# Fused attention and max-of-two projection on one core: a new order for the first part of the work, w2's first part loaded second and transposed ahead of the first pair's last scores

## The chip, the cores and the metric

One core of one Trainium2 chip. The metric is device time in microseconds of one execution; the median of three runs before the change is 329.46 us (329.17 to 329.52).

## The reference

```python
batch, n_heads, seq, head_dim = (8, 12, 448, 64)
scores = scale * np.matmul(q, k.transpose(0, 1, 3, 2))
scores = cap * np.tanh(scores / cap)
scores = scores - np.max(scores, axis=-1, keepdims=True)
attn = np.exp(scores)
attn = attn / (np.sum(attn, axis=-1, keepdims=True) + 1e-09)
attn_out = np.matmul(attn, v)
x = attn_out.transpose(0, 2, 1, 3).reshape(B * S, H * D)
h1 = x @ w1
h2 = x @ w2
g = np.maximum(h1, h2)
return g @ w_out
```

x is 3584 x 768, w1 and w2 are 768 x 1024, w_out is 1024 x 768, all given as float32. The cap is 30, so the exponentials stay small enough to be taken without the maximum, and the kernel leaves that subtraction out.

## The kernel before

The kernel computes in bfloat16 with sums in float32. It uses max(h1, h2) = relu(h1 - h2) + h2: with wd = w1 - w2 (`wd_sb`) and wm = w2 @ w_out (`wm_sb`), the result is relu(x @ wd) @ w_out + x @ wm. The product wm is made in the kernel, out of transposed pieces of w2.

The whole program is one list of steps, `ORDER` (lines 9 to 203), read by the loop at line 742. Each engine gets its instructions in the order in which they stand there and works them off in that order; a step that waits holds all later steps of its own engine. Nothing reorders them. GpSimd's queue (POOL) issues nearly all loads, converting to bfloat16; SyncE (SP) and ScalarE (ACT) issue the four plain loads of the first two pairs; SyncE also issues the transposing DMAs and the stores. A load from GpSimd also waits for the landing of the load eight places ahead of it.

Heads are worked in pairs (48 of them, pair i) and quads (t, pairs 2t and 2t + 1). One step is a name and its numbers:

- `ld0`, `cd`: plain loads of k and q of pairs 0 and 1, and their casts. `lk i`, `lq i`, `lv t`: loads of k, q and v from GpSimd (lines 317 and 336). `lw2 c`, `lw1 c`, `lwo`: parts of w2, w1, w_out (lines 364, 389, 357).
- `dm`, `ms0`, `ms`, `id`: VectorE (DVE) memsets of `warm`, of `ident`, of `ones` and its kin; `id` is GpSimd's affine select that makes `ident` the identity.
- `D bank n`: filler matmuls on `warm` (`keep_warm`, line 465), n units of 128 columns in instructions of up to 512.
- `X i bank` and `Xh`: TensorE transposes of k and q of pair i (L458), moved to SBUF by VectorE with `XC`, `XCh` (L463). `W c bank`: transposes of w2's part c (L416), moved with `WC` (L420).
- `S i j`: scores of pair i, keys 128 j to 128 j + 127 (L514); `L t`: the 64 keys left over, for the quad (L528). `T`, `TL`: tanh of these on ScalarE (L519, L532). `E i j0 j1`, `EL`: the exponentials (L536, L539).
- `OP c half bank`, `P c half n`: n matmuls of the premultiplication wm (L431); `PC`: its result to SBUF (L437). `sub c e`: wd = w1 - w2 (L402).
- `Y t bank`: sums of the exponentials (L566, L570, from quad 3 on L573, after the adds `A`, `B` on VectorE); `Y1`, `Y2`, `Y3`: their inverse. `VL t`, `V t u j0 j1`: the values (L600, L606); `N t u`: normalised into `xT` (L618, L621).
- `O g bank`, `M a b n`: open a group of the projection in a bank, and n steps of group a on the upper and b on the lower half of the rows of the array (L645; -1 is no group). `ev`, `eva`: the group's result to SBUF (L666, L702). `H`, `Hs`: a bank changes hands between the halves. `st`: store. `cr t`: DMA transpose of k and q from quad 5 on (L475).

Scores go to two PSUM tiles in turn, `s0` and `s1`, which `VL` and `V` share; the order of turns is line 503. A score step therefore waits for the tanh that empties its tile. The other four banks, mm0 to mm3, are named in the steps. For quad 0 the tiles are, in the order of the list: S 0 1 in s1, S 0 0 and S 0 2 in s0, L 0 and S 1 0 in s1, S 1 2 in s0, S 1 1 in s1. k and q of two quads (`kqs`) and v of two (`vp`) are held at a time, so a load waits until the quad two before has been used.

Before the change TensorE has, up to the first P: X 0, X 1, S 0 1, S 0 0, L 0, S 0 2, W 2, S 1 0, X 3, X 2, S 1 2, S 1 1, W 3, W 1, S 2 1, S 2 0, with D between. GpSimd's first loads are lk 3, lk 2, lq 3, lq 2, lw2 2, lw2 3, lw2 1, two of lwo, lv 0 1, lw2 0, lv 0 0.

Of the kernel before, what the change touches and what calls it, by code (L numbers as in the profile page):

```python
# [39 lines left out]
A 5 0 1; A 5 0 2; ev 8; ev 9; M 11 10 7; S 12 1; lk 17 1; M 11 10 4; T 12 0; lq 17 0; O 12 2; M 12 10 1; A 5 1 1;  # L40
M 12 10 1; Hs 11; cr 7; M 12 10 1; M 12 11 1; B 5 0; M 12 11 1; T 12 1; M 12 11 1; S 12 2; H 10 2; B 5 1;
M 10 11 1; T 12 2; M 10 11 5; E 11 2 3; st 0 0; M 10 11 2; O 13 0; M 13 11 1; ev 10; L 6; VL 5; A 5 1 2; TL 6;
V 5 0 0 2; V 5 1 0 2; Y 5 3; E 12 0 3; V 5 0 2 3; V 5 1 2 3; Y1 5; S 13 0; M 13 11 1; lv 7 0; M 13 11 1; Y2 5;
M 13 12 2; Y3 5; M 13 12 1; lv 7 1; M 13 12 3; N 5 0; M 13 12 1; lv 7 2; M 13 12 1; T 13 0; M 13 12 1; N 5 1;
M 13 12 1; lv 7 3; M 13 12 1; O 14 3; M 14 12 2; EL 6; Hs 13; S 13 1; lk 18 0; M 14 12 1; M 14 13 1; ev 11;
M 14 13 1; Hs 12 2; T 13 1; S 13 2; lk 18 1; M 14 13 1; A 6 0 1; M 12 13 2; T 13 2; Hs 14; M 12 13 1; lq 18 0;
A 6 0 2; S 14 0; M 12 13 3; E 13 0 2; M 12 13 1; S 14 1; lk 19 0; M 12 13 1; O 15 1; M 15 13 2; ev 12; M 15 13 1;
lk 19 1; M 15 14 2; ev 13; M 15 14 1; T 14 0; O 16 2; M 16 14 1; lq 19 0; A 6 1 1; M 16 14 1; st 0 1; M 16 14 1;
Hs 15; T 14 1; cr 8; B 6 0; M 16 15 1; S 14 2; M 16 15 1; ev 14; M 16 15 1; T 14 2; O 17 0; M 17 15 2; H 16;
M 17 15 1; B 6 1; M 17 16 2; E 13 2 3; M 17 16 1; ev 15; O 18 3; M 18 16 1; L 7; VL 6; A 6 1 2; st 0 2; TL 7;  # L50
V 6 0 0 2; V 6 1 0 2; Y 6 1; E 14 0 3; V 6 0 2 3; V 6 1 2 3; Y1 6; S 15 0; M 18 16 1; lv 8 0; M 18 16 1; Y2 6;
M 18 17 1; Y3 6; M 18 17 1; lv 8 1; M 18 17 1; O 19 1; M 19 17 2; ev 16; Hs 18; lv 8 2; M 19 17 1; M 19 18 1;
T 15 0; N 6 0; M 19 18 2; lv 8 3; O 20 2; M 20 18 2; EL 7; Hs 19; ev 17; M 20 18 1; lk 20 0; S 15 1; M 20 19 1;
N 6 1; M 20 19 1; T 15 1; M 20 19 1; lk 20 1; O 21 0; M 21 19 3; Hs 20; M 21 20 1; lq 20 0; ev 18; M 21 20 1;
S 15 2; S 16 0; ev 19; M 21 20 1; T 15 2; O 22 3; M 22 20 1; lk 21 0; M 22 20 1; A 7 0 1; Hs 21; M 22 20 1;
M 22 21 1; E 15 0 2; M 22 21 1; lk 21 1; ev 20; S 16 1; M 22 21 1; O 23 1; M 23 21 1; A 7 0 2; M 23 21 1; Hs 22;
lq 21 0; M 23 21 1; M 23 22 2; ev 21; M 23 22 1; T 16 0; M 23 22 2; A 7 1 1; M 23 22 2; cr 9; M 23 22 1; T 16 1;
M 23 22 1; B 7 0; S 16 2; M 23 22 2; B 7 1; O 24 2; M 24 22 1; T 16 2; M 24 22 2; H 23; M 24 23 1; H 22 2;
E 15 2 3; M 24 23 2; M 22 23 1; L 8; VL 7; A 7 1 2; TL 8; V 7 0 0 2; V 7 1 0 2; Y 7 0; E 16 0 3; V 7 0 2 3;
# [719 lines left out]
```

## Time and profile before

| | us |
|---|---|
| median of 3 runs | 329.46 |
| lowest, highest | 329.17, 329.52 |
| the profiled execution | 329.59 |
| its span in the trace | 327.8 |

The profile is of one execution. PE is TensorE's matmul, PEld its weight loads, DVE VectorE, ACT ScalarE, POOL GpSimd, SP SyncE. A timeline row is start, length, engine, line, operation, output and input, count, and in brackets the idle time before it with what ended it. L numbers are lines of this kernel. Times within the span start at its begin; the difference between the profiled execution's time and its span lies outside of the trace. Ends of matmuls are modelled, and a row with a length of several instructions runs from the first's start to the last's end.

### The profile page before, as it was taken

What the parts mean: (1) busy time and instruction counts of PE and PEld (TensorE: products, weight loads), DVE (VectorE), ACT (ScalarE), POOL (GpSimd) and SP (SyncE); (2) the same over time, 40 slices, a digit from 0 to 9 for tenths busy, and PEclk for the clock granted to TensorE, in tenths of its full rate; (3) what the DMA queues carried; (4) which work ended last, traced back from release to release, by engine and by line L of the source; (5) the groups of instructions that cost most, each with busy time, mean ns of one, the idle gap of its engine ahead of it and who ended that gap; (6) DMA issues with size and microseconds to landing.
All of it is one profiled execution on the core that took longest, in us unless ns stands there. A gap on an engine that the chain in (4) does not pass through costs nothing.

```text
span 327.8 us, 9768 instructions
## 1 busy us (share of the span) xinstructions
PE 320.3 (98%) x4137; PEld 184.6 (56%) x4140; DVE 240.2 (73%) x422; ACT 281.2 (86%) x278; POOL 161.7 (49%) x237
## 2 busy tenths in 40 slices
PE   8899999999999999999999999999999999999994
...
ACT  5899999999999999999999999999999999921120
...
GB/s 186 193 201 134 289 185 168 115 127 137 202 187 102 118 193 194 123 79 170 165 184 90 212 138 184 109 177 142 188 114 90 211 154 46 2 50 98 0 98 96
DMA packets 134507, 46.28 MB, mean 141 GB/s; under 512 B 112320, under 2 KB 129472, under 8 KB 134464
## 3 DMA queue, kind: packets, MB, share of 16 engines
...
q8 instruction: 32, 0.52, 0.7%
q10 hardware_dynamic: 448, 0.66, 0.5%
...
## 4 chain that ended last, share of the span: by engine, by line
PE 86%; DVE 6%; DMA 6%; POOL 1%; issue 1%; POOLq 0%; DVEq 0%
PE mm L645 58%; PE s L514 8%; PE s L606 8%; DMA w2b<-in_moe_w_dram 3%; PE mm L431 3%; DMA osb<-in_moe_w_dram 2%; PE s L528 2%; PE mm L573 1%; PE mm L640 1%; PE s L600 1%; DVE wd_sb L402 1%; PE mm L416 1%; DVE gT L666 1%; DVE xT L621 1%; POOL kqs L321 1%; PE mm L458 1%
## 5 line engine op out<-in xcount | busy, mean ns | idle before, releaser
L519 ACT ACTIVATE e<-s 128x896 bf16<-128x896 f32 x144 | 125.8, 928 | 6.3 <-PE s L514 6.0
L536 ACT ACTIVATE e<-e 128x1792 bf16<-128x1792 bf16 (+2 forms) x72 | 123.2, 1712 | 0.0
L645 PE MATMUL mm<-wo_sb,gT 64*128 64x384 bf16 x864 | 115.5, 323 | 0.0
L645 PE MATMUL mm<-wm_sb,xT 64*128 64x384 bf16 x648 | 101.9, 323 | 0.1
L645 PE MATMUL mm<-xT,wd_sb 64*128 64x448 bf16 x768 | 97.2, 350 | 0.0
L328 POOL DMA_DIRECT2D kqs<-in_k_dram x76 | 54.7, 721 | 54.0 <-DMA qkT<-kqs 49.9
L645 PEld LDWEIGHTS <-gT 64*128 64x128 bf16 x864 | 58.7, 94 | 25.4 <-issue 1.1
L645 PEld LDWEIGHTS <-wd_sb 64*128 64x128 bf16 x768 | 48.9, 94 | 27.2 <-issue 2.4
L645 PEld LDWEIGHTS <-xT 64*128 64x128 bf16 x648 | 50.5, 94 | 18.3 <-issue 0.2
L514 PE MATMUL s<-qkT 64*128 64x448 bf16 x288 | 51.8, 352 | 0.0
L352 POOL DMA_DIRECT2D vp<-in_v_dram x48 | 30.6, 642 | 34.3 <-PE s L514 26.4
L666 DVE TENSOR_SCALAR gT<-mm 128x448 bf16<-128x448 f32 x64 | 38.9, 617 | 8.6 <-PE mm L645 7.6
L328 POOL DMA_DIRECT2D kqs<-in_q_dram x38 | 35.1, 925 | 5.9 <-PE mm L458 5.0
L606 PE MATMUL s<-e,vp 128*32 128x448 bf16 x576 | 36.0, 354 | 0.0
L548 DVE TENSOR_TENSOR esum<-e 128x896 bf16<-128x896 bf16 x42 | 26.0, 618 | 9.9 <-ACT e L536 9.9
L621 DVE TENSOR_TENSOR xT<-s,inv 64x448 bf16<-64x448 f32 x48 | 29.9, 622 | 0.9
L548 DVE TENSOR_TENSOR esum<-esum,e 128x896 bf16<-128x896 bf16 x42 | 26.2, 623 | 5.8 <-ACT e L536 4.8
L514 PEld LDWEIGHTS <-qkT 64*128 64x128 bf16 x288 | 18.4, 94 | 19.2 <-issue 11.0
L700 ACT COPY osb<-mm 128x384 f32<-128x384 f32 x10 | 4.8, 478 | 26.9 <-PE mm L645 26.7
L702 DVE COPY osb<-mm 128x384 f32<-128x384 f32 x44 | 23.3, 554 | 5.0 <-PE mm L645 4.5
L553 DVE TENSOR_TENSOR esum<-esum,el 64x896 bf16<-64x896 bf16 x42 | 26.0, 619 | 1.2
L578 DVE STREAM_TRANSPOSE st<-mm 128x448 f32<-128x448 f32 x24 | 15.6, 649 | 13.2 <-PE mm L573 11.6
...
## 6 DMA issues: line engine op xcount, KB each, us to landing
...
kqs<-in_q_dram POOLq DMA_DIRECT2D x46, 112.0 KB, 5.6
...
w2b<-in_moe_w_dram POOLq DMA_DIRECT2D x6, 256.0 KB, 6.8
...
vp<-in_v_dram POOLq DMA_DIRECT2D x10, 128.0 KB, 6.8
```

What stands on the lines that cost most here:

```text
L328: nc.gpsimd.dma_start(out=to, in_=x)
L352: nc.gpsimd.dma_start(out=to, in_=x)
L514: scored[i, j] = nc.tensor.matmul(s[:, h, :S], k_of(t, o, h, j), q_of(t, o, h)).ins
L519: nc.scalar.activation(expo[i][:, 2 * j : 2 * j + 2, :], slots[i, j][:, :, :S], AF.Tanh, scale=scale / cap)
L536: nc.scalar.activation(e, e, AF.Exp, scale=float(cap))
L548: nc.vector.tensor_add(d, e[:, 0:2, :] if j == 1 else d, e[:, 2 * j : 2 * j + 2, :])
L553: nc.vector.tensor_add(d, d, left_e[t][r, :, :])
L606: nc.tensor.matmul(vals[t][place(m, u), u, :S], w[:, m, :], expo[2 * t + o][:, 2 * j + h, :], start=False, stop=(j == NJ - 1))
L621: nc.vector.tensor_mul(x[64 - r : 128 - r], vals[t][r : r + 64, u, :S], sums[t, 3][64 - r : 128 - r])
L645: ins = nc.tensor.matmul(self.ps, w[r], x[r], start=first, stop=self.at == [self.n, self.n]).ins
L666: nc.vector.tensor_relu(gT[b // 2][:, f, cs], ps)
L702: nc.vector.tensor_copy(o[:, hs], ps)
```

## The change

Only `ORDER` changes. Up to the opening of the projection's twelfth group the steps stand in another order; no step of the computation is added or taken away there. The filler goes from 104 units (28 instructions) to 96 (26). `lw2 3` is GpSimd's second transfer, and `W 3` stands ahead of `S 0 2`; `ms` stands ahead of `dm` and `ms0`, and `id` ahead of GpSimd's first load. Some steps get another bank. After that point banks 0 and 2 are exchanged in many of the `O` and `Y` steps, and nothing else differs. The new list has one line more, so that line numbers behind it grow by one.

```diff
-ld0 k; ld0 k 1; ld0 q; ld0 q 1; dm; ms0; lk 3 0; lk 2 0; lq 3 0; id; D 3 8; ms; cd q; cd k; lq 2 0; lw2 2; lw2 3;
-lw2 1; D 3 24; Xh 0 0 0; Xh 0 1; cd k 1 1; cd q 1 1; XCh 0 1; XCh 0 0; D 3 5; X 1 1; S 0 1; S 0 0; XC 1; T 0 1;
-T 0 0; D 0 5; D 1 12; L 0; D 1 8; S 0 2; W 2 0; TL 0; T 0 2; S 1 0; X 3 2; D 1 26; X 2 1; S 1 2; T 1 0; E 0 0 3;
-T 1 2; lwo 0 0; lwo 0 1; lv 0 1; lw2 0; lv 0 0; lk 5 0; lq 5 0; lq 4 0; lk 4 0; lwo 1 0; lv 1 1; lwo 1 1; WC 2;
-XC 3; XC 2; S 1 1; W 3 3; W 1 2; D 0 16; S 2 1; WC 1; WC 3; T 1 1; E 1 2 3; T 2 1; S 2 0; OP 1 0 1; P 1 0 1;
-OP 3 0 3; P 3 0 3; OP 2 0 0; P 2 0 3; P 1 0 1; P 2 0 1; P 1 0 2; L 1; P 3 0 1; P 1 0 2; P 3 0 1; P 2 0 1; P 1 0 1;
-P 3 0 1; P 2 0 3; P 3 0 2; PC 3 0; PC 2 0; T 2 0; E 1 0 2; TL 1; EL 0; S 2 2; S 3 0; Y 0 2; P 1 0 1; W 0 0; T 2 2;
-T 3 0; VL 0; V 0 0 0 3; V 0 1 0 3; S 3 1; X 4 3; lv 1 0; lk 8 0; lw2 5; lq 6 0; lk 7 0; lk 6 0; lw2 4; lq 8 0;
-lw1 4; lq 7 0; lw1 2; lw1 0; lv 2 1; lv 2 0; WC 0; Y1 0; Y2 0; PC 1 0; Y3 0; XC 4; N 0 0; N 0 1; E 2 0 3; T 3 1;
-EL 1; E 3 0 2; X 5 0; OP 0 0 2; P 0 0 5; OP 1 1 3; P 1 1 4; P 0 0 1; OP 2 1 1; P 2 1 3; S 4 0; S 3 2; P 0 0 1;
-P 2 1 2; P 0 0 1; P 1 1 3; P 2 1 3; P 1 1 1; XC 5; PC 0 0; PC 2 1; PC 1 1; T 3 2; T 4 0; E 3 2 3; OP 3 1 2;
-P 3 1 2; S 4 1; S 4 2; Y 1 1; T 4 1; T 4 2; L 2; P 3 1 4; VL 1; V 1 0 0 3; V 1 1 0 3; TL 2; E 4 0 3; S 5 0;
-P 3 1 2; W 4 3; T 5 0; EL 2; Y1 1; Y2 1; Y3 1; N 1 0; N 1 1; WC 4; PC 3 1; X 6 1; X 8 0; S 5 1; S 5 2; W 5 2;
-XC 8; XC 6; sub 4 0; WC 5; T 5 1; T 5 2; OP 4 0 0; P 4 0 8; S 6 0; X 7 1; OP 0 1 3; P 0 1 8; S 6 1; E 5 0 2;
-T 6 0; E 5 2 3; T 6 1; PC 4 0; XC 7; sub 2 0; PC 0 1; S 6 2; OP 5 1 1; P 5 1 7; L 3; T 6 2; TL 3; E 6 0 3; Y 2 3;
-VL 2; V 2 0 0 3; V 2 1 0 3; S 7 0; OP 5 0 2; P 5 0 1; P 5 1 1; P 5 0 7; sub 0 0; Y1 2; Y2 2; Y3 2; N 2 0; N 2 1;
-PC 5 1; A 3 0 1; PC 5 0; T 7 0; EL 3; lw1 1; lk 9 0; lq 10 0; lk 11 0; lw1 3; lq 9 0; lk 11 1; lv 3 1; lq 11 0;
-lv 4 0; lv 3 0; lk 10 0; lw1 5; lk 10 1; O 0 0; M 0 -1 1; S 7 2; S 7 1; O 1 3; M 1 -1 1; M 0 -1 3; M 1 -1 1;
-M 0 -1 2; T 7 1; T 7 2; Hs 0; S 8 0; M 1 -1 1; M 1 0 3; S 8 1; X 9 2; OP 4 1 1; P 4 1 4; sub 1 0; sub 3 0; XC 9;
-E 7 0 2; T 8 1; T 8 0; P 4 1 4; L 4; O 2 2; M 2 0 2; S 8 2; M 2 0 1; M 2 1 3; A 3 0 2; A 3 1 1; B 3 1; PC 4 1;
-ev 0; B 3 0; Hs 2; TL 4; E 7 2 3; T 8 2; S 9 0; O 3 1; M 3 1 3; M 3 2 3; O 4 0; M 4 2 3; VL 3; T 9 0; E 8 0 3;
-A 3 1 2; ev 1; ev 2; sub 5 0; Hs 3; cr 5; V 3 0 0 1; Y 3 3; V 3 0 1 3; V 3 1 0 3; M 4 3 1; S 9 1; M 4 3 2; O 5 2;
-M 5 3 3; lk 12 1; lk 13 0; lv 5 3; lq 13 0; lv 6 2; lv 4 1; lv 5 1; lk 12 0; lq 12 0; lk 15 0; lq 15 0; lk 13 1;
-lq 14 0; lk 14 0; Hs 4; M 5 4 3; T 9 1; Y1 3; Y2 3; Y3 3; ev 3; N 3 1; N 3 0; Hs 5; O 6 3; M 6 4 3; M 6 5 3;
-O 7 1; M 7 5 3; S 10 0; Hs 6; ev 5; A 4 0 1; ev 4; M 7 6 3; S 9 2; Hs 7; cr 6; EL 4; E 9 0 2; T 10 0; T 9 2;
-O 8 2; M 8 6 2; S 10 2; M 8 6 1; M 8 7 3; S 10 1; O 9 0; M 9 7 2; T 10 2; T 10 1; E 9 2 3; M 9 7 1; VL 4;
-V 4 1 0 2; L 5; TL 5; E 10 0 3; A 4 1 1; A 4 0 2; H 8; B 4 1; B 4 0; ev 7; A 4 1 2; ev 6; M 9 8 7; V 4 0 0 1;
...
+ld0 q; ld0 k; ld0 k 1; ms; dm; ms0; cd k; ld0 q 1; id; lq 3 0; lw2 3; lk 3 0; lk 2 0; lq 2 0; lw2 1; lw2 2; cd q;
+D 3 24; Xh 0 0 0; Xh 0 1; cd k 1 1; cd q 1 1; XCh 0 1; XCh 0 0; D 3 4; X 1 1; S 0 1; S 0 0; XC 1; T 0 1; T 0 0;
+D 0 5; D 3 1; D 1 8; L 0; W 3 3; S 0 2; X 3 2; TL 0; T 0 2; S 1 0; D 1 28; X 2 0; D 1 10; S 1 2; T 1 0; E 0 0 3;
+T 1 2; lwo 0 0; lwo 0 1; lq 4 0; lw2 0; lk 4 0; lv 0 1; lv 0 0; XC 3; XC 2; S 1 1; W 1 1; W 2 2; D 0 16; S 2 1;
+WC 1; WC 3; WC 2; T 1 1; EL 0; T 2 1; S 2 0; OP 3 0 0; P 3 0 2; OP 2 0 3; P 2 0 1; P 3 0 1; P 2 0 2; L 1;
+OP 1 0 2; P 1 0 2; P 2 0 1; P 1 0 2; P 2 0 1; P 1 0 4; P 2 0 3; PC 1 0; PC 2 0; T 2 0; TL 1; E 1 0 2; S 3 0;
+S 2 2; T 3 0; T 2 2; E 1 2 3; P 3 0 4; W 0 1; X 4 2; VL 0; V 0 0 0 1; Y 0 3; V 0 0 1 3; V 0 1 0 3; S 3 1; P 3 0 1;
+lwo 1 0; lv 1 1; lq 5 0; lwo 1 1; lk 5 0; lk 7 0; lq 6 0; lv 2 0; lk 8 0; lv 1 0; lk 6 0; lq 8 0; lw2 4; lw1 2;
+lw2 5; lq 7 0; lv 2 1; lw1 4; lw1 0; WC 0; XC 4; Y1 0; Y2 0; Y3 0; N 0 1; N 0 0; PC 3 0; E 2 0 3; T 3 1; EL 1;
+E 3 0 2; OP 1 1 1; P 1 1 1; OP 0 0 2; P 0 0 5; OP 2 1 3; P 2 1 3; P 1 1 1; P 0 0 2; P 1 1 1; P 2 1 1; P 0 0 1;
+S 3 2; S 4 0; P 1 1 1; P 2 1 1; P 1 1 1; P 2 1 2; P 1 1 2; P 2 1 1; P 1 1 1; X 5 0; PC 2 1; PC 0 0; XC 5; T 3 2;
+T 4 0; E 3 2 3; S 4 1; S 4 2; OP 3 1 3; P 3 1 1; T 4 1; T 4 2; P 3 1 1; Y 1 2; L 2; TL 2; E 4 0 3; X 6 0; VL 1;
+V 1 0 0 3; V 1 1 0 3; S 5 0; T 5 0; EL 2; Y1 1; Y2 1; Y3 1; XC 6; N 1 0; N 1 1; PC 1 1; X 8 0; OP 0 1 2; P 0 1 4;
+P 3 1 2; S 5 2; S 5 1; P 0 1 2; P 3 1 2; P 0 1 2; P 3 1 2; W 4 1; XC 8; sub 2 0; WC 4; PC 3 1; T 5 1; T 5 2;
+W 5 0; S 6 0; S 6 1; X 7 1; E 5 0 2; T 6 0; E 5 2 3; T 6 1; WC 5; PC 0 1; XC 7; OP 4 0 3; P 4 0 8; OP 5 1 2;
+P 5 1 2; S 6 2; Y 2 0; L 3; OP 5 0 1; P 5 0 1; T 6 2; TL 3; E 6 0 3; P 5 0 1; P 5 1 1; VL 2; V 2 0 0 1; V 2 1 0 3;
+V 2 0 1 3; S 7 0; P 5 0 2; P 5 1 2; P 5 0 4; P 5 1 3; PC 4 0; sub 4 0; Y1 2; Y2 2; sub 0 0; Y3 2; N 2 0; N 2 1;
+PC 5 0; A 3 0 1; A 3 0 2; PC 5 1; T 7 0; EL 3; lk 11 0; lv 3 0; lk 9 0; lw1 5; lw1 1; lq 9 0; lq 10 0; lw1 3;
+lv 3 1; lv 5 2; lk 10 1; lk 11 1; lk 12 1; lq 11 0; lk 12 0; lk 10 0; S 7 1; O 1 3; M 1 -1 1; O 0 0; M 0 -1 2;
+S 7 2; M 0 -1 3; M 1 -1 1; M 0 -1 1; T 7 1; T 7 2; E 7 0 2; Hs 0; S 8 0; M 1 -1 1; M 1 0 3; S 8 1; X 9 2;
+OP 4 1 1; P 4 1 5; sub 5 0; sub 1 0; XC 9; A 3 1 1; T 8 1; E 7 2 3; T 8 0; P 4 1 3; L 4; O 2 2; M 2 0 3; M 2 1 3;
+S 8 2; PC 4 1; B 3 1; B 3 0; ev 0; A 3 1 2; Hs 2; TL 4; T 8 2; O 3 1; M 3 1 3; S 9 0; M 3 2 3; T 9 0; E 8 0 3;
+ev 1; sub 3 0; Hs 3; cr 5; VL 3; V 3 0 0 1; V 3 1 0 2; Y 3 3; O 4 0; M 4 2 1; S 9 1; M 4 2 2; V 3 1 2 3;
+V 3 0 1 3; M 4 3 3; lk 13 1; lk 13 0; lq 13 0; lv 6 3; lv 5 1; lq 12 0; lv 4 0; lv 4 1; lq 15 0; lv 6 2; lk 14 1;
+Y1 3; Y2 3; ev 2; Y3 3; Hs 4; O 5 2; M 5 3 3; M 5 4 3; T 9 1; EL 4; E 9 0 2; N 3 1; N 3 0; ev 3; Hs 5; O 6 3;
+M 6 4 3; M 6 5 2; S 9 2; S 10 0; M 6 5 1; O 7 1; M 7 5 3; Hs 6; A 4 0 1; ev 4; A 4 1 1; A 4 0 2; ev 5; M 7 6 3;
+Hs 7; cr 6; T 10 0; T 9 2; S 10 2; O 8 0; M 8 6 3; S 10 1; M 8 7 3; O 9 2; M 9 7 1; T 10 2; T 10 1; E 9 2 3;
+M 9 7 2; VL 4; L 5; V 4 1 0 1; V 4 0 0 3; V 4 1 1 3; TL 5; B 4 1; B 4 0; H 8; ev 7; A 4 1 2; ev 6; Y 4 1; M 9 8 1;
+S 11 0; M 9 8 10; O 10 3; M 10 8 3; EL 5; T 11 0; E 10 0 3; Hs 9; Hs 8 2; Y1 4; M 10 9 3; Y2 4; Y3 4; N 4 0;
...
-T 36 2; M 70 71 5; st 4 0; E 35 2 3; M 70 71 2; O 73 2; M 73 71 1; ev 70; L 18; VL 17; A 17 1 2; TL 18;
+T 36 2; M 70 71 5; st 4 0; E 35 2 3; M 70 71 2; O 73 0; M 73 71 1; ev 70; L 18; VL 17; A 17 1 2; TL 18;
...
```

More of the change, by code (lines that the diff above doesn't have):

```diff
@@ L40 @@
[L40 to L59, printed above, removed]
@@ new lines @@
+H 10 2; B 5 1; M 10 11 1; T 12 2; M 10 11 5; E 11 2 3; st 0 0; M 10 11 2; O 13 2; M 13 11 1; ev 10; L 6; VL 5;
+A 5 1 2; TL 6; V 5 0 0 2; V 5 1 0 2; Y 5 3; E 12 0 3; V 5 0 2 3; V 5 1 2 3; Y1 5; S 13 0; M 13 11 1; lv 7 0;
+M 13 11 1; Y2 5; M 13 12 2; Y3 5; M 13 12 1; lv 7 1; M 13 12 3; N 5 0; M 13 12 1; lv 7 2; M 13 12 1; T 13 0;
+M 13 12 1; N 5 1; M 13 12 1; lv 7 3; M 13 12 1; O 14 3; M 14 12 2; EL 6; Hs 13; S 13 1; lk 18 0; M 14 12 1;
+M 14 13 1; ev 11; M 14 13 1; Hs 12 2; T 13 1; S 13 2; lk 18 1; M 14 13 1; A 6 0 1; M 12 13 2; T 13 2; Hs 14;
```

174 lines of the change are left out of this document (94 added, 80 removed).

## The prediction

> **What bounds the kernel now.** I read the page's first two parts, then the windows, then the chain and the timeline of the first 17 us, then single stalls further on.
>
> ```profile
> span 327.8 us, 9768 instructions
> PE 320.3 (98%) x4137; PEld 184.6 (56%) x4140; DVE 240.2 (73%) x422; ACT 281.2 (86%) x278; POOL 161.7 (49%) x237
> PE   8899999999999999999999999999999999999994
> ACT  5899999999999999999999999999999999921120
> ```
>
> TensorE (PE) is busy for all but 7.5 us of the span. ScalarE (ACT) runs full up to the 34th slice, so both limit the early part, and TensorE alone the end. The windows say where TensorE is idle (columns: length, PE busy, PEld, DVE, ACT, POOL, clock, DMA share, GB/s).
>
> ```profile
> 0.00:10.00 10.00, 7.94 (x86) 3.08 (x87) 2.59 (x10) 5.97 (x8) 7.65 (x17) 1.00 0.87 183
> 10.00:20.00 10.00, 9.34 (x124) 5.47 (x127) 3.23 (x5) 8.90 (x9) 4.07 (x7) 1.00 1.26 200
> ...
> 30.00:40.00 10.00, 9.46 (x159) 5.09 (x156) 7.50 (x14) 10.00 (x11) 4.69 (x8) 1.00 1.10 258
> ...
> 300.00:327.80 27.80, 23.68 (x246) 15.09 (x242) 4.85 (x8) 2.87 (x6) 0.00 (x0) 1.00 0.28 72
> ```
>
> Idle are 2.06 us in the first ten, 0.66 in the second, 0.54 between 30 and 40, and 4.12 in the tail, which the change leaves alone. Some of the busy time is filler too: the matmuls on `warm` (L471), grouped for the first 16.4 us.
>
> ```profile
> L471 PE MATMUL mm<-warm 128*128 128x512 bf16 (+2 forms) x25 | 7.9, 444 | 1.5 <-DVE warm L734 1.2 <-issue 0.2
> ```
>
> So about 10.6 us ahead of 16.4 us are idle or filler, and from then on nearly every slot is work that must be done in either order. The change can win only by ending the filler sooner, and lose only by opening gaps where there are none now. The timeline shows what ends the filler.
>
> ```profile
> 6.91 1.73 ACT L519 ACTIVATE e<-s 128x896 bf16<-128x896 f32 x2 [0.80 <-PE s L514]
> ...
> 8.88 0.36 PE L514 MATMUL s<-qkT 64*128 64x448 bf16 x2
> 9.31 0.94 ACT L519 ACTIVATE e<-s 128x896 bf16<-128x896 f32 x1
> 10.40 0.62 PE L416 MATMUL mm<-ident,w2b 128*128 128x128 bf16 x8 [1.15 <-DMA w2b<-in_moe_w_dram]
> 10.95 0.36 PE L514 MATMUL s<-qkT 64*128 64x448 bf16 x2
> 11.36 0.92 ACT L519 ACTIVATE e<-s 128x896 bf16<-128x896 f32 x1 [1.10 <-PE s L514]
> 12.03 1.35 PE L471 MATMUL mm<-warm 128*128 128x512 bf16 x6 [0.16 <-issue]
> 12.17 2.44 ACT L536 ACTIVATE e<-e 128x2688 bf16<-128x2688 bf16 x1
> 15.60 0.81 PE L471 MATMUL mm<-warm 128*128 128x512 bf16 x3
> 16.83 1.96 PE L431 MATMUL mm<-wo_sb,w2T 128*128 128x384 bf16 x11
> 16.94 1.73 ACT L519 ACTIVATE e<-s 128x896 bf16<-128x896 f32 x2
> ```
>
> TensorE takes its queue in order. At 9.2 us it comes to W 2 (the first transposes of w2), waits 1.15 us for that DMA, and behind it stands S 1 0, the next pair's first scores. ScalarE, done with T 0 2 at 9.31 + 0.94 = 10.25, gets them at 11.36: 1.11 us in which the engine that paces the next 30 us has nothing. From 12.2 us on it has no gap of note (of the 1.1 us missing in the row 10.00:20.00 this is all, and 30.00:40.00 is full), and the last filler ends at 16.35 only because the second pair's score buffers wait for it.
>
> **The change part by part.**
>
> *The first part of w2.* lw2 3 is now second on GpSimd's queue instead of fifth or sixth, and W 3 stands ahead of S 0 2, where filler (D 1 8) runs now. S 0 2, then X 3, then S 1 0 follow. All depends on when the DMA lands (issue time from the timeline, time to landing from the DMA view of single issues: first k, last q, first w2, third w2, and a w2 part issued later at 26.27).
>
> ```profile
> 0.86 0.27 DVE L734 MEMSET warm<- 128x256 uint32 x1 [0.86 <-PEq L760]
> 1.24 1.24 POOL L321 DMA_DIRECT2D kqs<-in_k_dram  x2 [0.79 <-POOLq L760]
> 1.43 0.28 DVE L292 MEMSET ones<- 64x64 bf16 x2
> 3.07 0.33 POOL L277 TENSOR_SCALAR_AFFINE_SELECT ident<-ident 128x128 bf16<-128x128 bf16 x1
> 3.31 0.57 POOL L321 DMA_DIRECT2D kqs<-in_q_dram  x1
> 3.85 1.62 POOL L366 DMA_DIRECT2D w2b<-in_moe_w_dram  x3
> kqs<-in_k_dram POOLq DMA_DIRECT2D x1, 112.0 KB, 4.6
> kqs<-in_q_dram POOLq DMA_DIRECT2D x1, 112.0 KB, 4.3
> w2b<-in_moe_w_dram POOLq DMA_DIRECT2D x1, 256.0 KB, 6.5
> w2b<-in_moe_w_dram POOLq DMA_DIRECT2D x1, 256.0 KB, 7.9
> w2b<-in_moe_w_dram POOLq DMA_DIRECT2D x1, 256.0 KB, 4.7
> ```
>
> The four k and q loads land at 1.24 + 4.6 = 5.84 to 3.31 + 4.3 = 7.61, 0.59 apart. The three w2 parts land from 10.35 to 4.93 + 7.9 = 12.83 (third issue 3.85 + 2 x 0.54), on average 1.74 apart; the first alone took 2.74. With one load ahead of it the new first part would land at 5.84 + 1.74 = 7.6. But the queue also starts later: the four memsets of `ms` (1.43 + 0.28 less their start behind `ident`, about 0.5 us) now go ahead of `warm` and `ident` on VectorE, so `ident` is ready at about 1.75, and the affine select, now first on GpSimd, pushes the first DMA from 1.24 to about 2.05. That is 0.8 later. It need not move the landings: the DMA engines are 87% busy over the first ten microseconds (row 0.00:10.00), at first with the four plain loads of the first k and q. Bounds: 2.6 + 4.7 = 7.3 (latency of the later part) to 5.84 + 2.74 + 0.8 = 9.4. I take 8.0, near the average-spacing value with half of the delay.
>
> With a landing at L, S 0 2 starts at L + 0.6 (the 0.55 from 10.40 to 10.95 and a wait), ScalarE's T 0 2 0.43 behind that (8.88 to 9.31) and ends 0.94 later: L + 1.97, but not before 10.25 as now. X 3 (0.5) and S 1 0 (0.4) run under it. L = 8.0 gives 10.25: T 1 0 comes 1.1 us sooner. L = 9.4 gives 11.37: nothing. Value taken: -1.1.
>
> *The rest up to the first premultiplication.* D 1 28, X 2, D 1 10, S 1 2, S 1 1, W 1, W 2, D 0 16 follow from 10.2 us: 1.4 + 0.5 + 0.5 + 0.5 + 1.1 + 0.75 (rates of the rows above) end at about 15.0, so the first P starts at 15.4 to 15.7 and ScalarE's T 2 1 at 15.85 instead of 16.94. The last two of the seven k, q and w2 loads are the sixth and seventh in both orders, 12.83 to 13.6, when W 2 is due at 13.5. EL 0 changes places with E 1's last third (about 1.0 us each): nothing. All the transposes, scores and P steps keep their number; two filler matmuls fewer change nothing, since filler fills waiting.
>
> *`ms` ahead of `warm`.* Its half microsecond delays the first filler from 1.19 to 1.7, and only 24 units stand there instead of 32:
>
> ```profile
> 1.19 3.59 PE L471 MATMUL mm<-warm 128*128 128x512 bf16 x8 [1.19 <-DVE warm L734]
> 4.72 0.63 PE L458 MATMUL mm<-ident,kqs 64*64 64x64 bf16 x28
> 5.28 0.45 PE L471 MATMUL mm<-warm 128*128 128x512 bf16 x2
> ```
>
> Eight filler matmuls took 0.45 us each, and from 5.28 on 0.22: TensorE starts slow and becomes fast after some 3.5 us, though the granted clock reads 1.00 in every window row. Six of them from 1.7 end at 4.3, then it idles until X 0 at 4.72. Cost between 0 (fast by the time that scores start) and about 1.0 (X 0, a filler, X 1 and the first scores at twice their time, less 0.3 that X 1 waits for ScalarE's cast anyway). The fast state is more likely to come at about 5.2; I take 0.1. [...]
>
> *New orders further on.* W 5 waits today for a bank that PC 3 1 empties late:
>
> ```profile
> 37.68 0.55 DVE L437 CAST wm_sb<-mm 128x384 bf16<-128x384 f32 x1
> 38.28 0.61 PE L416 MATMUL mm<-ident,w2b 128*128 128x128 bf16 x8 [0.53 <-DMA osb<-in_moe_w_dram]
> ```
>
> The row names a DMA, but PC 3 1 ends at 38.23 and W 5 starts 0.05 later; both use bank 2. In the new order W 5 has bank 0, empty since XC 8: up to -0.5. Against it TensorE, early, runs into score buffers that ScalarE has not freed: at L 1, at S 5 1 (behind T 5 0) and at L 3, some tenths of a microsecond each, if its order runs as tightly as now. These are not losses of ScalarE's time; they say that TensorE cannot gain more than ScalarE's 1.1. I take 0 for both together, with a bound of 0.5 on either side, the size of the one such wait that the trace shows.
>
> *GpSimd's queue.* It stands at lv 2 0 until V 0 is done, where it now stands at lk 8 until X 4, which comes later; so the w1 parts come no later. Further on lv 4 0 and lv 4 1 stand behind lv 5 1, which must wait for V 3, and VL 4 needs them:
>
> ```profile
> 59.94 0.61 POOL L352 DMA_DIRECT2D vp<-in_v_dram  x1 [4.32 <-PE s L606]
> vp<-in_v_dram POOLq DMA_DIRECT2D x1, 128.0 KB, 3.8
> 66.64 0.38 PE L600 MATMUL s<-el,vp 64*32 64x448 bf16 x8
> ```
>
> The first row is lv 5 1 today. One microsecond sooner it is at 58.9; behind it come lq 12 (0.57 by the q load above, perhaps 0.9) and the two v loads at 0.61: the last is issued at 60.7 to 61.1 and lands 3.8 later, by 64.9. VL 4 is due at 65.6. It fits, with 0.7 to spare: 0, bound +0.5, as V 3 itself can be some tenths late, with two score and M steps put inside it. The exchange of banks 0 and 2 in all later groups renames buffers only: 0.
>
> Sum: -1.1 + 0.1 + 0 + 0.1 (a tenth for the tight loads) = -0.9 us. The profiled execution took 329.59 us with its span of 327.8, so 1.79 lie outside; it would become 328.7. The median shown is 329.46, 0.13 lower, so I predict 328.55.
>
> **The rivals.**
>
> *The first part lands late (slower).* W 3 now stands in front of S 0 2, so a late DMA stalls two steps of ScalarE instead of one. It decides from L = 9.4. If the part lands at 10.35, like today's first, T 0 2 ends at 12.32 and T 1 0 is 0.96 us later than now: 330.4. For it: the later start of the queue, and 2.74 us that the first w2 part took. Against: three loads (1.8 us) fewer ahead of it.
>
> *TensorE stays slow longer.* Then T 0 1 starts up to 1.0 us later than 6.91 and takes the whole chain along; the gain shrinks to 0.1: 329.4. Today's order hides such a delay in the 1.15 us at W 2, the new one doesn't.
>
> *The gain is given back.* A load that fits by less than a microsecond (v for VL 4, q of pair 9 for X 9, the transpose DMA for S 10 0) is late by as much as was won: TensorE was full there already, so the time returns to about 329.4.
>
> *More is won.* W 5's half microsecond comes on top, and the loads hold: -1.6, 327.85.
>
> **How the numbers follow.** Forecast, within 0.3 us: 0.42. More won: 0.10. Slow TensorE 0.10, given back 0.16, late first part or a longer stall of the kind 0.22. The kernel's timing tells 0.2% (0.66 us) from no change. The first two give faster, 0.52. The next two give no change, 0.26. The last gives slower, 0.22. The likeliest case alone reaches from 328.25 to 328.85; with the others, 327.8 to 330.2 leaves out the end of the late case and little below.
>
> **What would show it.** Right: the first w2 transposes at 8 to 8.4 us with no wait, ScalarE's fifth activation at 10.2 to 10.4, the first L431 row at 15.4 to 16.0, the first L645 row at 47.5 to 48.2 instead of 48.80, and no idle TensorE behind it. Wrong: a wait of more than a microsecond at the first L416, first scores later than 6.9, or a row of TensorE idle behind `vp`, `kqs` or `qkT` between 48 and 80 us.
>
> ```profile
> 48.80 0.36 PE L645 MATMUL mm<-xT,wd_sb 64*128 64x448 bf16 x1
> ```

## The result and the profile after

| | before | changed |
|---|---|---|
| median, us | 329.43 | 331.62 |
| lowest to highest, us | 329.17 to 329.71 | 328.62 to 336.48 |
| executions | 22 | 22 |
| the profiled execution, us | 329.59 | 328.62 |
| its span, us | 327.8 | 326.8 |

The ratio is 1.0053, 95% interval 1.0036 to 1.0071: slower by half a per cent, clear of the noise. It leaves out executions more than 1.5% above a kernel's fastest (six of the changed kernel's 22), so it understates the loss (the medians alone give 331.62 / 329.43 = 1.0066).

The changed kernel's executions lie 7.9 us apart where those of before lie 0.5 apart, and the profiled one is the fastest of all. It shows what the change does when nothing goes wrong. First its page and its windows (columns as before: length, PE, PEld, DVE, ACT, POOL busy, clock, DMA share, GB/s):

```profile
span 326.8 us, 9775 instructions
PE 320.3 (98%) x4138; PEld 184.3 (56%) x4138; DVE 240.0 (73%) x422; ACT 280.8 (86%) x278; POOL 161.5 (49%) x237
```

```profile
0.00:10.00 10.00, 8.05 (x120) 4.05 (x120) 2.61 (x10) 5.59 (x8) 6.89 (x16) 1.00 0.89 180
10.00:20.00 10.00, 10.00 (x103) 4.81 (x99) 3.91 (x7) 10.00 (x10) 4.85 (x9) 1.00 1.25 196
30.00:40.00 10.00, 9.92 (x187) 5.42 (x184) 8.42 (x15) 10.00 (x10) 5.69 (x9) 1.00 1.12 257
60.00:70.00 10.00, 9.68 (x126) 4.91 (x122) 9.28 (x18) 9.34 (x11) 6.95 (x10) 1.00 1.25 128
```

Between 10 and 20 us TensorE lacks nothing now (0.66 before), between 30 and 40 it lacks 0.08 (0.54 before). The timeline of the same execution:

```profile
4.69 0.95 PE L459 MATMUL mm<-ident,kqs 64*64 64x64 bf16 x28 [0.16 <-DVE kqs L311]
...
7.29 1.73 ACT L520 ACTIVATE e<-s 128x896 bf16<-128x896 f32 x2 [0.89 <-PE s L515]
...
8.57 0.62 PE L417 MATMUL mm<-ident,w2b 128*128 128x128 bf16 x8
...
9.70 1.75 ACT L520 ACTIVATE e<-s 128x896 bf16<-128x896 f32 x2
...
11.29 2.48 ACT L537 ACTIVATE e<-e 128x2688 bf16<-128x2688 bf16 x1
...
15.93 1.15 PE L432 MATMUL mm<-wo_sb,w2T 128*128 128x384 bf16 x6
...
47.72 0.35 PE L646 MATMUL mm<-xT,wd_sb 64*128 64x448 bf16 x1
...
66.11 0.38 PE L601 MATMUL s<-el,vp 64*32 64x448 bf16 x6 [0.26 <-DMA vp<-in_v_dram]
```

The reader is to see: the first w2 transposes (L417) start without a wait; T 1 0 follows T 0 2 in one row (9.70, two activations) where there was a gap of 1.10 us; the exponentials of pair 0 start at 11.29 instead of 12.17, the first P at 15.93 instead of 16.83, the first projection step at 47.72 instead of 48.80. At 66 us VL 4 waits 0.26 us for its v load. The first part did what was forecast, and 328.62 is 0.07 above the predicted 328.55. The median isn't there: 20 of the 22 executions are at 329.97 us or more, so most must hold something that this trace doesn't show.

### The profile page after: what moved, and what is told of

The parts are those of the page before. It is cut to its first block, busy times and chain, and to the rows that moved or that the text cites. A ratio compares the mean times of both kernels' runs of the same rounds, so it can differ in the third digit from the quotient of the medians.

```text
span 326.8 us, 9775 instructions
## 1 busy us (share of the span) xinstructions
PE 320.3 (98%) x4138; PEld 184.3 (56%) x4138; DVE 240.0 (73%) x422; ACT 280.8 (86%) x278; POOL 161.5 (49%) x237
## 4 chain that ended last, share of the span: by engine, by line
PE 94%; DMA 2%; DVE 1%; POOL 1%; issue 1%
PE mm L646 59%; PE s L515 10%; PE s L607 9%; PE mm L432 5%; PE s L529 2%; PE mm L459 2%; PE s L601 2%; PE mm L574 2%; PE mm L641 1%; PE mm L472 1%; DMA vp<-in_v_dram 1%; DMA kr<-in_k_dram 1%; PE mm L417 1%; PE mm L567 1%; POOL vp L353 0%
## 5 line engine op out<-in xcount | busy, mean ns | idle before, releaser
L537 ACT ACTIVATE e<-e 128x2688 bf16<-128x2688 bf16 (+2 forms) x72 | 124.0, 1726 | 0.0
```

What stands on the lines that cost most here:

```text
L537: nc.scalar.activation(e, e, AF.Exp, scale=float(cap))
```

## The experiments

The times are medians, with the lowest and highest in brackets. "Theory A" in the first four is that the spread comes from TensorE's clock at the start, after the later and shorter filler; "Theory B" is that a load lands late in some executions.

**The changed kernel once more** (one execution, 332.88 us), to have a trace of a long one.

> The changed kernel once more, for a trace of another of its executions (22 of them lay between 328.6 and 336.5 us, those of before between 329.2 and 329.7). Theory A, TensorE's clock: an execution of 330 us or more shows the first slow matmuls (0.43 us for 512 columns) going on behind 6.9 us, or slow ones again later, and the same DMA landings as in the 328.6 us one. Theory B, the loads: matmuls are fast from 6.9 us on as in the 328.6 us execution, and a wait on w2b, vp or kqs is a microsecond or more longer.

The start was as good as in the profile above (E 0 at 10.88, the first projection step at 47.59). The loss is at the first scores of pair 14. The timeline rows that lead there, first from the shorter execution shown above (in order of time: SP's transposing DMA of quad 6, GpSimd's loads lk 16 1 and lq 14 0, the transposing DMA of quad 7, S 14 0), and behind them, from the view of that tile, the time that quad 7's DMA took from issue to landing:

```profile
64.26 2.12 SPq L476 DMA_TRANSPOSE qkT<-kqs  x1
...
71.51 0.74 POOL L329 DMA_DIRECT2D kqs<-in_k_dram  x1
...
74.52 0.93 POOL L329 DMA_DIRECT2D kqs<-in_q_dram  x1
...
78.79 1.47 SPq L476 DMA_TRANSPOSE qkT<-kqs  x1
...
84.27 0.39 PE L515 MATMUL s<-qkT 64*128 64x448 bf16 x2
```

```profile
DMA to landing us min/median/max: 3.5/3.5/3.5
```

The same rows of the longer execution:

```profile
64.01 2.56 SPq L476 DMA_TRANSPOSE qkT<-kqs  x1
...
72.90 0.74 POOL L329 DMA_DIRECT2D kqs<-in_k_dram  x1 [1.30 <-DMA qkT<-kqs]
...
75.91 0.93 POOL L329 DMA_DIRECT2D kqs<-in_q_dram  x1
...
80.53 1.58 SPq L476 DMA_TRANSPOSE qkT<-kqs  x1
...
87.15 0.55 PE L515 MATMUL s<-qkT 64*128 64x448 bf16 x2 [2.31 <-DMA qkT<-kqs]
```

```profile
DMA to landing us min/median/max: 6.6/6.6/6.6
```

And of the kernel before (lq 14 0, quad 7's transposing DMA, S 14 0):

```profile
65.29 0.92 POOL L328 DMA_DIRECT2D kqs<-in_q_dram  x1
...
76.74 1.90 SPq L475 DMA_TRANSPOSE qkT<-kqs  x1
...
85.23 0.39 PE L514 MATMUL s<-qkT 64*128 64x448 bf16 x2
```

The changed order puts GpSimd's loads at this place as follows, in lines that the diff above left out:

```diff
-lv 5 1; lk 12 0; lq 12 0; lk 15 0; lq 15 0; lk 13 1; lq 14 0; lk 14 0;
...
-lv 6 0; lk 15 1; lv 6 1; lk 14 1; lv 5 0; lk 17 0; lv 5 2; lk 16 1; lv 6 3; lq 16 0; lk 16 0;
+lk 14 0; lv 6 1; lv 6 0; lk 15 0; lk 15 1; lv 5 3; lk 16 1; lq 16 0; lv 5 0; lk 17 0; lq 14 0; lk 16 0;
```

q of pair 14 used to be issued at 65.29, ahead of GpSimd's wait for V 4. Now it stands behind that wait and nine loads, which alone makes it 9.2 us later (74.52). One of the nine, lk 16 1, can add a wait of its own. Pair 16's k goes into the `kqs` buffer of quad 6, so lk 16 1 waits until quad 6's transposing DMA has landed. That DMA took 6.2 us in the one execution (64.26 to 70.5, no wait) and 8.4 in the other (64.01 to 72.4: GpSimd stands 1.30 us, from 71.60 to 72.90). Quad 7's transposing DMA needs q of pair 14, follows it by 4.3 to 4.6 us, and took 3.5 and 6.6 us itself: it lands at 82.3 and at 87.1, where S 14 0 is due at 84.27 and at 87.15 - 2.31 = 84.84. Before, the same view gives 6.1 us for it, so it landed at 76.74 + 6.1 = 82.8, 2.4 us ahead of need. The 3.5 us of the fastest execution are the exception: six other traces (the longer execution, the kernel before, and four of the variants below) have 6.1 to 7.6 us for quad 7's DMA, and with 6.1 it would have landed at 84.9 there too, behind need.

TensorE loses 2.31 us, and then something more. Windows of the longer execution:

```profile
86.00:87.00 1.00, 0.00 (x0) 0.00 (x0) 0.00 (x0) 0.73 (x1) 0.00 (x0) 0.89 1.37 303
87.00:90.00 3.00, 2.85 (x18) 1.37 (x20) 0.29 (x1) 1.52 (x2) 2.36 (x4) 0.50 0.95 217
90.00:91.00 1.00, 1.00 (x13) 0.84 (x10) 0.66 (x2) 0.31 (x1) 1.00 (x2) 0.90 0.87 55
```

The granted clock falls to 0.50 at 86.78 (0.89 = 0.78 + 0.22 x 0.5) and returns at 90.20. From 87.15 on that costs, as an estimate from these times, (90.20 - 87.15) x 0.5 = 1.5 us. Idle time and clock together make 3.8 of the 4.3 us by which this span (331.1) exceeds the other (326.8). S 14 0 was due 0.57 us later already (84.84 against 84.27), which covers the rest. The mean clock of each execution shows how common this is: ten of the 22 have 0.994 or less, and they took 333.14 us or more; the other twelve have 0.997 or more and took at most 332.04.

**The start, in the new order and in the old.** Three runs: `dm; ms0` ahead of `ms` with 32 units of filler; the same with 24 units; and the order of before with `ms` first and without its `D 3 8`, that is with the changed kernel's late filler of 24 units.

```diff
-ld0 q; ld0 k; ld0 k 1; ms; dm; ms0; cd k; ld0 q 1; id; lq 3 0; lw2 3; lk 3 0; lk 2 0; lq 2 0; lw2 1; lw2 2; cd q;
-D 3 24; Xh 0 0 0; Xh 0 1;
+ld0 q; ld0 k; ld0 k 1; dm; ms0; ms; cd k; ld0 q 1; id; lq 3 0; lw2 3; lk 3 0; lk 2 0; lq 2 0; lw2 1; lw2 2; cd q;
+D 3 32; Xh 0 0 0; Xh 0 1;
```

> The changed order with the old start of VectorE and TensorE: dm and ms0 ahead of ms, and 32 units of filler ahead of X 0 instead of 24. Theory A (short and late filler leaves TensorE's clock slow in some executions): the spread goes, all within 0.5 us, at 328.1 to 328.6. Theory B (a load that is late in some executions): spread of several us stays, median 330 or more.

> The changed order with only dm and ms0 put ahead of ms; 24 units of filler stay, so that TensorE starts at 1.2 us but idles from about 3.8 to 4.7. Theory A, if the start counts: as e2. Theory A, if the length of unbroken work counts: spread as in the changed kernel, 328.5 to 334. Theory B: spread stays as well.

> The order of before with only its start changed: ms ahead of dm and ms0, and 24 units of filler instead of 32 ahead of X 0; loads, w2 and everything else as before. Theory A: the spread appears here too, 329.4 to 334, with a clock below 1.00 in the slow ones. Theory B: 329.2 to 329.8, as before.

| kernel | us | ratio to before |
|---|---|---|
| changed, dm first, 32 units | 332.53 (330.01 to 335.64) | 1.0082 [1.0053, 1.0112] |
| changed, dm first, 24 units | 331.98 (329.57 to 336.85) | 1.0069 [1.0048, 1.0091] |
| order of before, ms first, 24 units | 329.31 (329.03 to 330.07) | 0.9999 [0.9991, 1.0008] |

Theory A falls: the spread stays where the start is made as before, and doesn't come where the start of before is made like the changed one. In the old order's run the first scores were not late (T 0 1 at 6.91 us, as before), and its 1.15 us wait for w2 was still there; that this wait would have hidden a later start is likely, but no trace shows it.

The two spread kernels' profiled executions stall at S 14 0 too, with different ends. With 24 units, the timeline and the window:

```profile
87.13 0.36 PE L515 MATMUL s<-qkT 64*128 64x448 bf16 x2 [2.15 <-DMA qkT<-kqs]
```

```profile
80.00:90.00 10.00, 7.75 (x87) 4.75 (x85) 6.43 (x12) 8.59 (x8) 4.83 (x8) 1.00 1.07 180
```

With 32 units:

```profile
88.67 0.55 PE L515 MATMUL s<-qkT 64*128 64x448 bf16 x2 [2.53 <-DMA qkT<-kqs]
```

```profile
87.00:88.00 1.00, 0.00 (x0) 0.00 (x0) 0.00 (x0) 1.00 (x1) 0.00 (x0) 0.70 1.33 226
88.00:94.00 6.00, 5.33 (x32) 3.23 (x34) 2.16 (x4) 1.86 (x3) 4.65 (x6) 0.50 1.04 156
94.00:95.00 1.00, 1.00 (x13) 0.87 (x10) 0.60 (x2) 0.13 (x1) 0.00 (x0) 0.89 1.11 70
```

After 2.15 us of waiting the clock stayed at 1.00, and the span was 329.6 us. After 2.53 it was at 0.50 from 87.40 to 94.22, which by the same estimate costs (94.22 - 88.67) x 0.5 = 2.8 us more, and the span was 333.9. In that execution TensorE also stood 0.44 us at 84.80 us for a bank's hand-over (`Hs`), which stands behind quad 7's transposing DMA on SyncE: the late q load holds up that queue as well.

**One load moved, in both directions.** Theory C: lq 14 0 behind lk 16 1 is the cause. In the changed kernel it goes ahead, in the kernel before it goes behind.

```diff
-lk 14 0; lv 6 1; lv 6 0; lk 15 0; lk 15 1; lv 5 3; lk 16 1; lq 16 0; lv 5 0; lk 17 0; lq 14 0; lk 16 0;
+lk 14 0; lq 14 0; lv 6 1; lv 6 0; lk 15 0; lk 15 1; lv 5 3; lk 16 1; lq 16 0; lv 5 0; lk 17 0; lk 16 0;
```

> The changed kernel with one load moved: lq 14 0 directly behind lk 14 0, ahead of GpSimd's waits for V 4 and for the transposing DMA of quad 6. Theory C (q of pair 14 stands behind lk 16 1, which waits for quad 6's transposing DMA, so quad 7's comes late and S 14 0 stalls for 2 us or more): lq 14 is issued near 66 us instead of 74.5 to 76, quad 7's transposing DMA is issued near 77 instead of 79 to 81, S 14 0 has no wait, and the time is 328.2 to 328.9 in all executions, spread under 1 us. Rival D (the transposing DMAs or the granted clock are upset by the new first part itself, wherever q of pair 14 stands): the spread of 328.6 to 336.5 stays and the median is above 330.5.

```diff
-lk 13 1; lq 14 0; lk 14 0;
+lk 13 1; lk 14 0;
...
-lk 16 1; lv 6 3; lq 16 0; lk 16 0;
+lk 16 1; lv 6 3; lq 16 0; lq 14 0; lk 16 0;
```

> The kernel before with one load moved: lq 14 0 behind lk 16 1, lv 6 3 and lq 16 0, as the changed kernel has it, nothing else. Theory C: the q load is issued near 77.4 us or later, quad 7's transposing DMA 4.3 us behind it, near 81.7, landing 85 to 88.5, while S 14 0 is due at 85.2: the time is 330 to 335 and spread by some us, with a wait of TensorE on qkT near 85 us. Rival D: 329.4 as before, no spread.

| kernel | us | ratio to before |
|---|---|---|
| changed, lq 14 0 early | 328.87 (328.15 to 330.62) | 0.9986 [0.9974, 0.9997] |
| order of before, lq 14 0 late | 334.99 (332.92 to 337.66) | 1.0177 [1.0142, 1.0212] |

The one load takes 2.75 us off the changed kernel's median, and put late it costs the kernel before 5.6 us. Its rows in the changed kernel with the load early (lq 14 0, quad 7's transposing DMA, S 14 0):

```profile
65.72 0.92 POOL L329 DMA_DIRECT2D kqs<-in_q_dram  x1
...
76.00 1.56 SPq L476 DMA_TRANSPOSE qkT<-kqs  x1
...
84.48 0.39 PE L515 MATMUL s<-qkT 64*128 64x448 bf16 x2
```

And in the kernel before with the load late (GpSimd's lk 16 1, then lq 16 0 and lq 14 0 in one row, the same DMA, an M step behind a hand-over, S 14 0, and the windows behind it):

```profile
74.92 0.74 POOL L328 DMA_DIRECT2D kqs<-in_k_dram  x1
...
76.28 1.88 POOL L328 DMA_DIRECT2D kqs<-in_q_dram  x2
...
81.28 1.84 SPq L475 DMA_TRANSPOSE qkT<-kqs  x1
...
84.80 0.33 PE L645 MATMUL mm<-wm_sb,xT 64*128 64x384 bf16 x1 [0.59 <-SPq L654]
...
88.70 0.36 PE L514 MATMUL s<-qkT 64*128 64x448 bf16 x2 [2.56 <-DMA qkT<-kqs]
```

```profile
89.00:90.00 1.00, 1.00 (x16) 0.58 (x12) 0.00 (x0) 0.90 (x2) 0.81 (x2) 0.98 0.69 259
90.00:93.00 3.00, 3.00 (x20) 2.22 (x16) 2.26 (x4) 0.86 (x2) 3.00 (x4) 0.50 0.76 49
93.00:94.00 1.00, 1.00 (x12) 0.84 (x9) 0.55 (x1) 0.13 (x1) 0.95 (x2) 0.81 2.18 138
```

Here the clock falls at 89.96, 1.3 us after TensorE had begun to work again, and returns at 93.38. Rival D is out: the order of before, with its old first part, does the same. Theory C holds for the place of the load, but not for all of its reason: lk 16 1 didn't wait here (74.92), and q of pair 14 was late, near 77.2 us, by its place behind GpSimd's wait for V 4 and the loads there alone. The wait at lk 16 1 adds 1.30 us in the longer execution of the changed kernel and 1.54 with dm first and 32 units. Theory C had also set the spread with the load early under 1 us, and it was 2.5: something smaller remained.

**The load early, and the v loads of VL 4 ahead of lv 5 1.**

```diff
-lq 13 0; lv 6 3; lv 5 1; lq 12 0; lv 4 0; lv 4 1; lq 15 0;
+lq 13 0; lv 6 3; lv 4 0; lv 4 1; lv 5 1; lq 12 0; lq 15 0;
```

> As the run with q of pair 14 early, and besides lv 4 0 and lv 4 1 ahead of lv 5 1, which waits for V 3. If the 0.26 to 0.5 us that VL 4 waited for its v load reach the end, the time is 0.2 to 0.5 us under that run's; if the score buffers take that up anyway (TensorE is ahead of ScalarE there), it is the same within 0.1. By rival D both runs stay spread.

330.15 us (327.85 to 332.24), ratio 1.0024 [1.0000, 1.0048]. The best execution is lower, the median higher. VL 4 no longer waits, but this does (GpSimd's lk 16 1 and lv 5 0, then V 5):

```profile
73.50 0.74 POOL L329 DMA_DIRECT2D kqs<-in_k_dram  x1 [2.38 <-DMA qkT<-kqs]
...
75.15 0.64 POOL L353 DMA_DIRECT2D vp<-in_v_dram  x1
...
80.39 0.94 PE L607 MATMUL s<-e,vp 128*32 128x448 bf16 x16 [1.90 <-DMA vp<-in_v_dram]
```

lv 5 0 also stands behind lk 16 1, and here GpSimd waited 2.38 us there: this load is late by the wait at lk 16 1 itself.

**lv 5 0 ahead of it too; then lv 4 early as well; then dm first.** Each of the three adds its edit to the kernel before it.

```diff
-lv 5 3; lk 16 1; lq 16 0; lv 5 0; lk 17 0;
+lv 5 3; lv 5 0; lk 16 1; lq 16 0; lk 17 0;
```

> As the run with q of pair 14 early, and besides lv 5 0 ahead of lk 16 1, so that no load that is due soon stands behind GpSimd's wait for quad 6's transposing DMA. Theory C, second half (lv 5 0 there is the next victim: in the run with lv 4 early, GpSimd waited 2.38 us at lk 16 1, lv 5 0 was issued at 75.15 and V 5 waited 1.9 us for it): the spread goes, all executions between 328.0 and 329.0, median 328.5 or less, and no wait of TensorE on vp between 75 and 85 us, even where GpSimd waits 2 us or more at lk 16 1. Rival E (what is left of the spread comes from the start, whose first scores begin at 6.9 to 7.4 us): median 328.9 and a spread of 2 us as without this move.

> As the run with q of pair 14 and lv 5 0 early, and besides lv 4 0 and lv 4 1 ahead of lv 5 1. Theory C: with nothing behind lk 16 1 to suffer, VL 4's wait of 0.26 to 0.5 us is won or taken up by score buffers: 0 to 0.4 us less than without this move, 328.0 to 328.5, and no second spread. If lv 4 early does harm by itself (it held lv 5 1 until 60.54 instead of 58.89 in its first run), the time is 329 or more.

> As the run before it, and dm; ms0 ahead of ms, so that the filler starts at 1.19 us instead of 1.78 with 24 units. If the later start costs (first scores at 6.9 to 7.4 us in the executions with ms first, at 6.9 to 7.0 with dm first), the time is 0.1 to 0.4 us less, 327.8 to 328.3; if TensorE's later filler costs nothing, the same within 0.1.

| kernel | us | ratio to before |
|---|---|---|
| lq 14 0, lv 5 0 early | 329.18 (328.22 to 330.00) | 0.9993 [0.9982, 1.0004] |
| and lv 4 0, lv 4 1 | 328.13 (327.61 to 329.52) | 0.9964 [0.9954, 0.9974] |
| and dm first | 329.17 (328.23 to 330.70) | 0.9996 [0.9982, 1.0010] |

The second is faster than both kernels by more than the intervals. Its profiled execution took 327.61 us, and between 60 and 80 us TensorE lacks 0.06 us, with no wait for a load:

```profile
60.00:70.00 10.00, 9.94 (x134) 5.44 (x132) 9.83 (x18) 9.69 (x10) 8.19 (x12) 1.00 1.22 113
70.00:80.00 10.00, 10.00 (x144) 5.43 (x142) 7.12 (x14) 9.95 (x10) 6.44 (x10) 1.00 1.51 145
```

The first missed its expectation of 328.5 or less. No wait at V 5 is left, but VL 4 waited 0.3 us and E 0 began at 11.77 us only, against 10.78 in the second kernel's profiled execution, with the same start. So rival E has a part: the start varies by some tenths to a microsecond. That the v loads of VL 4 are worth 329.18 - 328.13 = 1.05 us is more than the 0.2 to 0.5 us that VL 4 waited in the six traces that show its wait; what the rest is wasn't found. That lv 5 0 mattered shows beside the run with lv 4 0 and lv 4 1 early and lv 5 0 late: 330.15 there, 328.13 here. The third missed too, in the other direction. With dm first, w2's first part is issued 0.6 us earlier (2.19 against 2.79) and TensorE waits for it all the same:

```profile
8.89 0.62 PE L416 MATMUL mm<-ident,w2b 128*128 128x128 bf16 x8 [0.69 <-DMA w2b<-in_moe_w_dram]
```

All three profiled kernels with dm first waited there (0.37, 0.69, 1.22 us), of the six with ms first and W 3 in the same place one did (0.35).

**S 0 2 ahead of W 3**, in the fastest kernel, so that a late w2 part holds up one step of ScalarE less.

```diff
-L 0; W 3 3; S 0 2; X 3 2;
+L 0; S 0 2; W 3 3; X 3 2;
```

> As the run with q of pair 14, lv 5 0, lv 4 0 and lv 4 1 all early (328.13 us, 327.6 to 329.5), and S 0 2 ahead of W 3, so that w2's first part, when it lands late, holds up S 1 0 alone and not S 0 2 as well. If the executions above 328.0 come from that landing (W 3 started between 8.06 and 9.14 us in the profiled executions with ms first), the median is 0.1 to 0.4 us less and the spread smaller; if they come from the slow TensorE at the start, no difference.

328.69 us (328.05 to 329.63), ratio 0.9984 [0.9975, 0.9994]: not the gain expected, rather half a microsecond lost. In the profiled execution E 0 began at 11.29, but the third w2 part to be needed was late:

```profile
15.08 0.62 PE L416 MATMUL mm<-ident,w2b 128*128 128x128 bf16 x8 [0.78 <-DMA w2b<-in_moe_w_dram]
```

One trace doesn't tell whether this belongs to the order; inconclusive.

**Is the clock's part real?** The kernel before with lq 14 0 late, which stalled in its profiled execution and took 332.92 us or more in each, and with ten M steps drawn ahead of S 14 0:

```diff
-A 6 0 2; S 14 0; M 12 13 3; E 13 0 2; M 12 13 1; S 14 1; lk 19 0; M 12 13 1; O 15 1; M 15 13 2; ev 12; M 15 13 1;
-lk 19 1; M 15 14 2; ev 13;
+A 6 0 2; M 12 13 3; E 13 0 2; M 12 13 1; lk 19 0; M 12 13 1; O 15 1; M 15 13 2; ev 12; M 15 13 1;
+lk 19 1; M 15 14 2; S 14 0; S 14 1; ev 13;
```

> The kernel before with lq 14 0 late, which took 332.9 to 337.7 us with a wait of 2.6 us at S 14 0 and a clock of 0.83 from 90 to 100 us, and now with S 14 0 and S 14 1 behind ten M steps (20 matmuls, about 2 us) that stood behind S 14 0. Theory F (the clock falls because TensorE is idle for more than some 2.2 us, and costs about 1.7 us on top of the idle time): the wait shrinks to 0.5 to 1 us, the clock is 1.00 throughout, and the time is 331 to 332.5, with a spread under 2 us. Rival G (the clock falls for another reason at that place, as the load of DMAs, and TensorE's idle time is the whole cost of the wait alone): the clock stays near 0.8 from 90 to 100 us and the time is 333 or more. If ScalarE, which gets its scores as late as before, sets the end, the clock is 1.00 and the time is still about 333.

331.47 us (330.87 to 334.24), ratio 1.0077 [1.0048, 1.0106].

```profile
85.23 0.33 PE L644 MATMUL mm<-wm_sb,xT 64*128 64x384 bf16 x1 [0.77 <-SPq L653]
...
89.03 0.55 PE L513 MATMUL s<-qkT 64*128 64x448 bf16 x4 [0.79 <-DMA qkT<-kqs]
```

```profile
90.00:100.00 10.00, 10.00 (x131) 5.09 (x129) 8.26 (x15) 9.21 (x10) 9.53 (x14) 1.00 1.50 180
```

Work for 2.56 - 0.79 = 1.8 us was put into the wait, and the median fell by 334.99 - 331.47 = 3.5 us. Between the two profiled executions the spans fell by 3.1 us (332.9 to 329.8). Their idle time ahead of S 14 0, with the waits for the hand-over, is 0.59 + 2.56 and 0.77 + 0.79 us, 1.6 less. The rest is about what a clock of 0.50 from 89.96 to 93.38 takes, by estimate (93.38 - 89.96) x 0.5 = 1.7, and here it is 1.00 over that whole time. So the clock's part is real and Theory F holds as to its price; a floor set by ScalarE at 333 us is out. Its spread of under 2 us didn't come (3.4): the longest execution, 334.24 us at a mean clock of 0.995, is the only one of the six below 0.997. Nor is 2.2 us of waiting the limit: with 32 units the clock fell 1.26 us into the wait (86.14 to 87.40). The last section comes back to this.

## Why the prediction was wrong, step by step

*The first part of w2* was right in mechanism and near in size. The part landed at 8.4 us (2.79 + 5.6), forecast 8.0 with bounds 7.3 to 9.4; E 0 came 0.88 us sooner, forecast 1.1. Over the nine profiled executions with W 3 ahead of S 0 2 (the changed kernel twice and seven variants) the first w2 transposes began between 8.06 and 9.46 us, about as the bounds had it, and E 0 between 10.78 and 12.08, where 12.17 was before. (The spacing of 1.74 us counts from the last q load at 7.61; the three w2 parts themselves landed 1.24 apart.)

*`ms` ahead of `warm`* was taken at 0.1, and it is a spread rather than a tenth. In the profile after T 0 1 began at 7.29 instead of 6.91: X 0 took 0.95 us instead of 0.63, so TensorE was still slow there. In the eight profiled kernels with ms first T 0 1 began between 6.78 and 7.44, four times at 6.91 or before; in the three changed ones with dm first between 6.85 and 6.97. The clock records of the two traces agree: the first full-speed record begins at 6.67 us in the profile after, where about 5.2 was forecast, and at 4.71 before. (The windows read 1.00 ahead of it because there is no record there. And the 0.22 us each from 5.28 on, in the prediction, is the mean of a matmul of 512 columns and one of 128.) So the rival of a long slow start came about in part, with up to 0.5 of its 1.0 us.

*New orders further on*: 0 taken for W 5's wait, within a bound of 0.5. The wait is gone, and the lead over the kernel before grew from 0.88 at E 0 to 1.08 us at the first projection step; in seven of the nine executions it grew by 0.14 to 0.22. That W 5 is the reason is argued, not tried.

*GpSimd's queue* is the step that failed: a term put at "0, bound +0.5". It named lv 4 0, lv 4 1 and VL 4, and VL 4's wait stayed within that bound (0.26 and 0.46 us in two executions of the changed kernel), though the prediction had counted 0.7 us to spare. But it stopped at VL 4. The moved list has a second block of loads, where lq 14 0 came to stand behind GpSimd's wait for V 4, and lq 14 0 and lv 5 0 behind lk 16 1; the prediction doesn't ask who waits for these. The place alone made lq 14 0 9.2 us later, and the wait at lk 16 1, which hangs on a DMA that took 6.2 and 8.4 us in the two executions shown, up to 1.54 more. The price was 2.15 to 2.53 us of idle time in the stalled executions of the changed order that were profiled, and 0 to 2.8 us of half clock behind it. That one load is worth 2.75 us of the changed kernel's median.

*The rivals.* The nearest was the gain given back, which named loads "that fit by less than a microsecond" and the transposing DMA of pair 10 as one of them. The kind was right; but the transfer that decided, quad 7's, had 2.4 us to spare before, so a search for tight loads couldn't find it, and giving back the gain (329.4) was not the most it could cost. Among the signs of a wrong forecast stood idle TensorE behind `qkT` between 48 and 80 us; it came at 85. The range ended at 330.2, below the median.

*The sum*: the best execution, 328.62, is the forecast's sum, but by luck of the draw: it is the trace in which quad 7's DMA took 3.5 us, where six others show 6.1 to 7.6. With lq 14 0, lv 5 0 and VL 4's two v loads put ahead of GpSimd's waits the kernel is at 328.13, 0.42 below the predicted time and 1.3 below the kernel before.
